# Decode attention on one core: sixteen deferred P V chunks instead of twenty, the next K asked for after piece 9 instead of 13, and wo's last heads ordered by halves

## The chip, the cores and the metric

One core of a Trainium2 chip. The metric is the device time of the whole kernel in microseconds (us), the slowest core's, as a median of several executions. The kernel before takes 1298.5 us; its executions differ by 0.6 us in the first comparison and by up to 2 us in the later ones, so differences of 1 us are read from the traces rather than from the times. Kernels are compared only within the same rounds.

## The reference, cut to what matters

```python
# B, Sq, D = 4, 1, 512;  H, Sk, Dh = 32, 8192, 128;  F = 1792;  all bf16
xn = layernorm(x)
q = (xn @ wq)                                   # [B, H, 1, Dh]
p = softmax(einsum("bhqd,bhkd->bhqk", q, k_cache) * Dh ** -0.5)
o = einsum("bhqk,bhkd->bhqd", p, v_cache)
y = x + o.reshape(B, 1, H * Dh) @ wo + (silu(xn @ w_gate) * (xn @ w_up)) @ w_down
```

K and V are 268 MB each, every byte is used once, and the rest (wq, wo, the three FFN weights) is 14 MB. 551 MB go from HBM to the core whatever the schedule.

## The kernel before

The (b, h) pairs are cut into 32 tiles of four heads. A tile's K is 8.4 MB, its V too, and three slots of that size hold K of the tile at work, V of the one before, and V of the one before that until its last chunk is used; then that slot is free for the next K. All loads go out on SyncE's queue, one DMA for a K or a V.

```python
def t_piece(n, g, jb):      # VectorE: 512 words of K transposed in 32x32 blocks
    kt = kt_pool.tile([P, w // 2], dt.bfloat16, name="kt")         # 3 buffers
    nc.vector.transpose(out=kt[:]..., in_=src[:, :, jb, :])
def s_piece(n, g, jb):      # PE: two matmuls, scores accumulate in PSUM
    for r in range(2):
        mm(s_ps[n][:], zq[:, 2 * jb + r, off:off + P], kt[:, :, r], start=...)
...
for i in range(NT - 1):
    for p in pieces(i, 0, NP):                   # 32 pieces: K of tile i
        if i >= 3 and p in (4, 7, 10, 13):
            pv_to(i - 2, NK - LO + (p - 1) // 3 * (LO // 4))   # LO = 20 chunks left of 64
            if p == 13:
                load_k(i + 1)                    # into V(i-2)'s slot
        if p == 16 and i > 0:
            pt_turn(i - 1)                       # VectorE: 4 transposes of P
    load_v(i)                                    # into K(i)'s slot
    max_1(i); build_q(i + 1)
    pv_to(i - 1, 8); max_2(i)
    ...                                          # each 4th tile: head group closed
    pv_to(i - 1, NK - LO); row_sums(i)
```

A piece is one such transpose with its two matmuls, 32 to a tile; a chunk is one P V matmul, 64 to a tile. `load_k` goes out when the slot is free, that is when PE has done the last P V chunk of two tiles before; where it stands in the program only bounds it.

## Time and profile before

| | before |
|---|---|
| time, median | 1298.5 us (4 runs) |
| DMA busy share, data queue q1 | 99.0% |
| mean rate | 425 GB/s |
| PE / VectorE busy | 85% / 63% |
| data moved | 551 MB |

From the page: the rate in 40 slices, the mean, and the chain of work that ended last; and from the waits, the sum of VectorE's waits for K (total us, times, longest).

```profile
GB/s 420 421 429 445 425 437 431 433 429 435 425 431 423 437 418 427 427 413 443 421 428 427 439 425 419 431 421 437 433 417 429 433 427 431 425 435 429 427 413 309
DMA packets 12612, 551.59 MB, mean 425 GB/s; under 512 B 1276, under 2 KB 1800, under 8 KB 3080
...
DMA 59%; PE 35%; DVE 4%; issue 2%; SPq 0%; ACT 0%; DVEq 0%
```

```profile
DVE kt L278 <- DMA slot<-in_A_k_cache_dram: 55.4, 27, 11.4
```

The rate never leaves 413 to 445 GB/s until the last slice; nothing in it looks like a pause. What 1% can hide is seen only in the records of single DMA packets (start, length, size, queue). Those records do not name the DMA engine.

### The profile page before, as it was taken

The page shows a single profiled execution, that of the slowest core. Times are in us where ns is not written, and L with a number is a line of the kernel's source. Part 1 is how long each engine was busy: PE and PEld are TensorE (multiplying, and loading weights), DVE is VectorE, ACT ScalarE, POOL GpSimd, SP SyncE. Part 2 cuts the span into 40 slices and gives each one's busy share as a digit, 9 for nine tenths or more (in the row PEclk, how much of TensorE's full clock was granted, in tenths as well). Part 3 has the DMA queues.
Part 4 walks back from the last instruction along what each step waited for, and adds up shares of the span by engine and source line. Part 5 has one row for each costly group of instructions (what it writes and reads, how often), then busy time and mean ns, then how long its engine had stood idle before and what let it go on. Part 6 is the DMA issues. An engine that isn't in the chain of part 4 may idle for free.

```text
span 1297.1 us, 12866 instructions
## 1 busy us (share of the span) xinstructions
PE 1099.1 (85%) x5010; PEld 441.8 (34%) x5076; DVE 823.0 (63%) x1509; ACT 34.1 (3%) x79; POOL 3.6 (0%) x11
## 2 busy tenths in 40 slices
PE   1888898988898978888988989878889888889887
PEld 0234333323333323333333333323333233333246
DVE  3956556676557676466776656766566775667753
ACT  1000000000000000000000000000000000000000
POOL 1000000000000000000000000000000000000000
PEclk8897999989989989899989989989999999999887
DMA  9999999999999999999999999999999999999997
GB/s 420 421 429 445 425 437 431 433 429 435 425 431 423 437 418 427 427 413 443 421 428 427 439 425 419 431 421 437 433 417 429 433 427 431 425 435 429 427 413 309
DMA packets 12612, 551.59 MB, mean 425 GB/s; under 512 B 1276, under 2 KB 1800, under 8 KB 3080
## 3 DMA queue, kind: packets, MB, share of 16 engines
q1 hardware_dynamic: 12536, 550.77, 99.0%
q8 instruction: 39, 0.64, 0.2%
q14 instruction: 21, 0.17, 0.0%
q10 hardware_dynamic: 16, 0.01, 0.0%
HBM read 550.77 MB, written 0.00 MB: 425 GB/s over the span
## 4 chain that ended last, share of the span: by engine, by line
DMA 59%; PE 35%; DVE 4%; issue 2%; SPq 0%; ACT 0%; DVEq 0%
DMA slot<-in_A_k_cache_dram 57%; PE sps L75 19%; PE oacc L75 14%; DVE kt L278 4%; DMA slot<-in_A_v_cache_dram 1%; PE mps L75 1%; DVE ptz L315 1%; PE yo_ps L75 1%; PE xps L75 1%; SPq L107 0%; ACT p__385 L306 0%; PE mps L297 0%; DVE rcp L325 0%; DVE mx L291 0%; DVE zq L269 0%
## 5 line engine op out<-in xcount | busy, mean ns | idle before, releaser
L75 PE MATMUL sps<-kt,zq 128*128 128x512 bf16 x1982 | 597.2, 421 | 172.9 <-DVE kt L278 172.3
L278 DVE STREAM_TRANSPOSE kt<-slot 128x512 uint32<-128x512 uint32 x1024 | 639.1, 681 | 152.2 <-PE sps L75 79.7
L75 PE MATMUL oacc<-slot,ptz 128*16 128x512 bf16 x1920 | 457.9, 387 | 0.0
L75 PEld LDWEIGHTS <-zq 128*128 128x128 bf16 x2048 | 202.1, 103 | 542.5 <-issue 397.5
L75 PEld LDWEIGHTS <-ptz 128*16 128x16 bf16 x1920 | 188.9, 107 | 250.1 <-issue 78.0
L325 DVE RECIPROCAL rcp<-mps 128x4 f32<-128x4 f32 x32 | 5.9, 185 | 198.3 <-PE mps L75 198.3
L291 DVE TENSOR_REDUCE mx<-sps 128x1 f32<-128x512 f32 x32 | 22.1, 692 | 23.1 <-PE sps L75 23.1
L75 PEld LDWEIGHTS <-slot 128*128 128x128 bf16 (+1 forms) x658 | 23.3, 110 | 11.6 <-DMA slot<-in_A_v_cache_dram 4.0
L300 DVE TENSOR_REDUCE nm<-mps 128x4 f32<-128x64 f32 x32 | 7.2, 225 | 24.1 <-PE mps L297 24.0
L269 DVE COPY zq<-qt 32x4 bf16<-32x4 bf16 x128 | 21.2, 166 | 1.3
L75 PE MATMUL xps<-ptz,slot 128*128 128x4 bf16 x512 | 15.6, 169 | 3.7 <-DMA slot<-in_A_v_cache_dram 3.7
L371 DVE TENSOR_TENSOR otn<-xps,rcp 32x16 bf16<-32x16 f32 x28 | 4.8, 170 | 21.4 <-PE xps L75 19.3
L75 PEld LDWEIGHTS mps<-rowb,rs 128*128 128x128 f32 x64 | 9.5, 187 | 14.7 <-issue 12.7
L75 PE MATMUL mps<-rowb,rs 128*128 128x4 f32 x64 | 12.3, 263 | 1.7 <-ACT p__385 L306 1.7
L349 DVE TENSOR_TENSOR kt<-kt,rowu 128x512 f32<-128x512 f32 x8 | 5.5, 693 | 10.2 <-ACT kt L348 10.1
L297 PE MATMUL mps<-ident_f,mx 128*128 128x128 f32 x32 | 10.3, 322 | 0.8 <-DVE mx L291 0.8
L75 PEld LDWEIGHTS xps<-rowy,o 128*32 128x32 f32 (+1 forms) x226 | 10.5, 155 | 1.3
L75 PE MATMUL xps<-rowy,o 128*32 128x4 f32 (+1 forms) x226 | 10.3, 203 | 0.0
L297 PEld LDWEIGHTS mps<-ident_f,mx 128*128 128x128 f32 x32 | 4.2, 133 | 13.9 <-DVE zq L269 12.5
L351 DVE TENSOR_REDUCE o<-kt 128x128 f32<-128x512 f32 x8 | 8.3, 1039 | 0.3
L75 PE MATMUL yo_ps<-slot,otn 128*4 128x256 bf16 x64 | 8.1, 290 | 0.3 <-DVE otn L361 0.3
L75 PE MATMUL sps<-slot,xnt_w 128*32 128x512 bf16 x32 | 3.5, 612 | 4.4 <-DMA slot<-in_A_wq_dram 4.4
(148 smaller groups left out, 184.1 us busy)
## 6 DMA issues: line engine op xcount, KB each, us to landing
slot<-in_A_v_cache_dram SPq DMA_DIRECT2D x6, 2048.0 KB, 26.4
slot<-in_A_wq_dram SPq DMA_DIRECT2D x1, 4096.0 KB
slot<-in_A_wo_dram SPq DMA_DIRECT2D x1, 3584.0 KB, 25.8
slot<-in_B_w_gate_dram SPq DMA_DIRECT2D x1, 1792.0 KB, 23.9
slot<-in_B_w_up_dram SPq DMA_DIRECT2D x1, 1792.0 KB, 27.8
slot<-in_B_w_down_dram SPq DMA_DIRECT2D x1, 1792.0 KB, 31.5
slot<-in_A_v_cache_dram SPq DMA_DIRECT2D x1, 1536.0 KB, 14.0
slot<-in_A_v_cache_dram SPq DMA_DIRECT2D x1, 1024.0 KB, 16.1
```

What stands on the lines that cost most here:

```text
L75: nc.tensor.matmul(out_ap, lhsT=lhsT, rhs=rhs, start=start, stop=True, skip_group_check=True, **kw)
L269: nc.vector.tensor_copy(out=zq[a * QB:(a + 1) * QB, :, XO + a * QB].rearrange("p (j r) -> p r j", r=2), in_=qt[a * QB:(a + 1) * QB, half, ...
L278: nc.vector.transpose(out=kt[:].bitcast(dt.uint32).rearrange("p (t r) -> p t r", r=QB), in_=src[:, :, jb, :])
L291: nc.vector.reduce_max(out=mx[:], in_=s_ps[n][:], axis=AX.X)
L297: nc.tensor.matmul(mps[:, 0:P], lhsT=nmx.pop(n)[:, 0:1].to_broadcast([P, P]), rhs=ident_f[:, :], is_transpose=True, start=True, stop=True, ...
L300: nc.vector.tensor_reduce(out=nm[:], in_=by_row(mps[:, 0:P]), axis=AX.X, op=ALU.max, negate=True)
L315: nc.vector.transpose(out=t_[y * QB:(y + 1) * QB, :, y, :, :].rearrange("p s u x -> p s (u x)"), in_=p_[y * QB:(y + 1) * QB, :].rearrange( ...
L325: nc.vector.reciprocal(out=rcp[j][:, :, b], in_=mps[:, P:P + HT])
L349: nc.vector.tensor_tensor(out=o_sb[:], in0=o_sb[:], in1=rowu[:].unsqueeze(2).to_broadcast([P, NV, Dh]), op=ALU.mult)
L351: nc.vector.reduce_sum(out=o1[:], in_=o_sb[:].rearrange("p u d -> p d u"), axis=AX.X)
L371: nc.vector.tensor_tensor(out=otn[q0:q1, j * 4:j * 4 + 4, :], in0=xps[q0:q1], in1=r_[q0:q1, y, :].unsqueeze(1).to_broadcast([QB, 4, B]), o ...
```

## The change

Its intent: the next K is asked for earlier in each tile, so that the DMA queue is never short, and the end is reached sooner because one half of the result is complete earlier.

```diff
-    def wo_mm(i):
-        for half in range(2):
+    def wo_mm(i, halves=(0, 1)):
+        for half in halves:
             mm(yo_ps[half][0:B, :], otn[:, i, :], wo_t[0][...], start=False)
-    LO = 20
+    LO = 16
-            if i >= 3 and p in (4, 7, 10, 13):
-                pv_to(i - 2, NK - LO + (p - 1) // 3 * (LO // 4))
-                if p == 13:
+            if i >= 3 and p in (3, 5, 7, 9):
+                pv_to(i - 2, NK - LO + (p - 1) // 2 * (LO // 4))
+                if p == 9:
                     load_k(i + 1)
-            if p == 16 and i > 0:
+            if p == 12 and i > 0:
                 pt_turn(i - 1)
...
-    wo_ready = H
-    wo_some(H)
-    assert wo_next == H
+    for half in range(2):
+        for h in range(JL * HT, H):
+            wo_mm(h, (half,))
+    assert wo_next == JL * HT
```

## The prediction

> **What bounds the kernel now.** The page's slices come first. DMA is at nine tenths or more in 39 of 40 slices, and PE and DVE are not.
>
> ```profile
> PE   1888898988898978888988989878889888889887
> DVE  3956556676557676466776656766566775667753
> DMA  9999999999999999999999999999999999999997
> ...
> q1 hardware_dynamic: 12536, 550.77, 99.0%
> q8 instruction: 39, 0.64, 0.2%
> q14 instruction: 21, 0.17, 0.0%
> ```
>
> The data queue q1 alone takes 99.0% of 16 engines' span, so all that can be won is in the last per cent: the start, the tail, and places where a DMA engine is slow or has nothing. The chain of waits names K transfers for 57% of the span, but it would do so whether the transfer or its request is late. So I went to the stretch of one tile, first the DMA requests (SyncE's timeline: start, length), then VectorE's wait for K in the same stretch:
>
> ```profile
> 550.24 0.33 SPq L94 DMA_DIRECT2D slot<-in_A_k_cache_dram  x1
> 562.83 0.33 SPq L107 DMA_DIRECT2D slot<-in_A_v_cache_dram  x1
> 588.39 0.33 SPq L94 DMA_DIRECT2D slot<-in_A_k_cache_dram  x1
> 601.71 0.33 SPq L107 DMA_DIRECT2D slot<-in_A_v_cache_dram  x1
> 628.50 0.33 SPq L94 DMA_DIRECT2D slot<-in_A_k_cache_dram  x1
> ...
> 576.05 4.27 DVE L278 STREAM_TRANSPOSE kt<-slot 128x512 uint32<-128x512 uint32 x7 [1.02 <-DMA slot<-in_A_k_cache_dram]
> 614.66 4.31 DVE L278 STREAM_TRANSPOSE kt<-slot 128x512 uint32<-128x512 uint32 x7 [1.78 <-DMA slot<-in_A_k_cache_dram]
> 654.29 4.89 DVE L278 STREAM_TRANSPOSE kt<-slot 128x512 uint32<-128x512 uint32 x7 [2.04 <-DMA slot<-in_A_k_cache_dram]
> ```
>
> The tile period is 38.6 to 39.6 us and VectorE waits 1 to 2 us for K in each, so compute is not the limit. The K landed at 614.66; the V asked for at 601.71 lies behind it and needs some 19.3 us more, until 634. The next K is asked for at 628.50, 5.5 us before that. The V at 601.71 was asked 13 us before its turn. So **only the K requests run near empty**.
>
> The records of single DMA packets say what this costs. A 64 KB packet takes 2.418 us at best, and that is also the median; one engine moves 8 of them per K or V, 19.32 us. Above that minimum, and including gaps, the K windows (from a K request to the next V request) from 157 us on lose 11.9 us per engine on average. It depends on the time from K's arrival to the next K request: 12.3 us loses 0 to 0.14, 13.8 loses 0.5 to 0.8, 14.5 loses 1.3 to 1.7 (the request at 550.24 loses 1.7, that at 588.39 nothing). It looks like a gain of 11 us.
>
> It is not, because **the engines don't run alike**. A transfer's 16 completion records lie 0.8 us apart for the first K, 3 to 4.6 us from 180 us on. I took the third K's 16 completions as zero and subtracted 19.32 us per transfer. After 58 transfers (to K 31) the earliest completion has lost 15.2 us, the last 17.9 us. The earliest loses nearly all of it in K transfers after late requests. The last loses it in 17 steps, most of 0.9 us, one to each of the 8 KB packets of q14 (about one in 66 us): 14.8 us, and q14's packets lie there also where no K is late. Of the other 3.1 us, 1.9 fall in K transfers with a late request (0.5, 0.8, 0.1, 0.2, 0.3) and 1.2 elsewhere. A slot is only ready when the last engine is, so the last engine's 1.9 us are the loss that the time sees; what the others win only puts them further ahead of it.
>
> **What the Trainium skill says.** "DMA: Bandwidth & Descriptors", Specifications, gives a fabric ceiling of 435 GB/s for 16 engines. The trace agrees: 64 KB in 2.418 us on 16 engines are 434 GB/s, and the mean is 425. The same page, "Why a DMA increments its semaphore by 16 and not by 1", says a DMA runs on up to 16 engines "that finish independently", and that only the full count means all data landed; the spread of 0.8 to 4.6 us shows it. Its section "Queues, rings and completion order" says each engine has a ring per queue row, and goes round the rows packet by packet; that fits an instruction packet delaying one engine's data, as the 0.9 us steps suggest. The page "Trainium Kernel Development and Optimization", Key Constraints, says all issuing queues share the same 16 engines, so asking earlier adds no bandwidth; here the busy share of 99% leaves none.
>
> **The change, part by part.** No instruction is added or removed: PE has 9582 rows in both programs, VectorE 336 merged rows in both.
>
> 1. *P V chunks.* Twenty deferred chunks become 16, so four move from a tile's start to the stretch after the previous tile's max. A run of 36 takes 7.96 us, 0.22 each: the stretch grows by 0.9 us. PE's idle before K at 614.66 was 2.77 us, so it is hidden in most tiles; in the one tile in four that closes a head group, whose next tile starts with no wait for K (at 417.83), it delays the start by up to 0.9.
>
> 2. *K's request.* Before, it comes after 13 pieces and 20 chunks: 628.50 - 614.66 = 13.84 us. Now it is after 9 pieces and 16 chunks. The tile's own lines say what a group costs:
>
> ```profile
> 623.09 1.53 PE L75 MATMUL sps<-kt,zq 128*128 128x512 bf16 x6
> 623.75 1.90 DVE L278 STREAM_TRANSPOSE kt<-slot 128x512 uint32<-128x512 uint32 x3 [0.76 <-PE sps L75]
> 624.55 1.26 PE L75 MATMUL oacc<-slot,ptz 128*16 128x512 bf16 x5
> 625.74 1.02 PEld L75 LDWEIGHTS <-zq 128*128 128x128 bf16 x6 [0.42 <-issue]
> ```
>
> Three pieces and five chunks take 625.74 - 623.09 = 2.65 us, about 1.4 + 1.25. Two pieces and four chunks are thus 0.93 + 1.0 = 1.95 us. Three first pieces at 2.8, four chunks at the low clock seen there (2.32 us for five) 1.8, then three groups of 1.95: 10.4 us. So the request comes about 3.4 us earlier after K's arrival. By the table above, 12.3 us was already early enough at a spread of 4 us; at 10.4 us the engines may draw some 7 us apart (4.2 + 13.8 - 10.4 = 7.6) before the fastest waits as at 13.8.
>
> 3. *V's request.* The transpose of P moves from piece 16 to 12 at the same cost (2.85 us on VectorE). Four pieces fewer are slowed by chunks, but the 0.9 us of part 1 is paid elsewhere. V comes perhaps 1 us earlier, where it was 13 us ahead anyway: zero.
>
> 4. *wo by halves.* The last eight matmuls are reordered, so that half 0 is done after four of them. The tail before:
>
> ```profile
> 1292.69 1.86 PE L75 MATMUL yo_ps<-slot,otn 128*4 128x256 bf16 x8 [0.27 <-DVE otn L361]
> 1294.38 0.41 DVE L474 CAST kt<-yo_ps 4x256 bf16<-4x256 f32 x1 [1.74 <-PE yo_ps L75]
> 1294.60 0.36 ACT L476 CAST kt<-yo_ps 4x256 bf16<-4x256 f32 x1 [18.41 <-PE yo_ps L75]
> 1294.82 0.35 SPq L475 DMA_DIRECT2D out_dram<-kt  x1
> 1294.99 0.28 ACTq L477 DMA_DIRECT2D out_dram<-kt  x1
> ```
>
> The VectorE cast and its store start three matmuls earlier, some 3 x 0.2 = 0.6 us. The ScalarE half still waits for the eighth matmul and its store was already the later one, at 1294.99. The end follows that one: 0 to 0.3 us, say 0.1.
>
> The sum: -1.9 (last engine's late-K loss) - 0.1 (tail) = -2.0, so 1298.4 - 2.0 = **1296.4 us**.
>
> **The rivals.** *Request bound:* the K request sets the pace for all engines, and the whole 11.9 us less a remainder of 1 us come back: 1287.5. For it: the 1.7 us at 550.24, the 57% of the chain. Against: the last engine's steps go with q14, not with K's request, and the earliest engine's gain is worth nothing if the last is as late. I give it one chance in ten; half of it, one in seven.
> *Fully hidden:* the slow engine pays q14's packets and nothing else, my 1.9 us are its neighbours' waits: 1298.3. For it: the five steps are small and I can't follow single engines through the records. One in five.
> *Compute takes over:* PE is at 85%, and the tiles that close a head group start without a wait for K (417.83 in VectorE's timeline), so 0.9 us more P V ahead of them, in 7 tiles, could add up to 6 us in all. Against: such a tile is followed by three with 1 to 3 us of wait, V is queued 13 us deep, and the K request in it still comes 2 us earlier than before. It would make 1299 to 1302; one in twenty.
>
> **Range and chances.** The three runs before span 0.6 us. Between hidden (1298.3) and half of the request-bound gain (1293) lies most of the weight: 1292.8 to 1298.7. Faster by over 2% would need 1272.5; 551 MB at 434 GB/s take 1270 us with nothing lost, and some 6 us of tail follow, so that is out of reach. Slower by 2% would need 26 us that nothing here can supply.
>
> **What would show it.** K's request about 10.4 us after K's arrival (13.8 before); V's request within 1 us of before. Slow 64 KB packets after K requests nearly gone; the spread of completions grown from 4 to 6 us or more; VectorE's waits for K (55.4 us before) about the same or longer, since DMA stays the bound; DMA's share no lower than 99%. The last engine's 0.9 us steps stay. In the tail the first cast about 0.6 us before the second. The prediction is wrong if the spread stays at 4 us while the time falls by 5 us or more (the request paced all engines), or if the waits for K vanish (compute took over).

## The result, and the profile after

| | before | after |
|---|---|---|
| first comparison, median | 1298.54 us (4 runs) | 1298.08 us (1297.41 to 1298.92, 4 runs) |
| repeated with five rounds, median | 1299.21 us (9 runs) | 1297.58 us (5 runs) |

Ratios are the mean time of one kernel's runs over that of the other's in the same rounds, so not quite the ratio of the medians: 0.9996 (95% interval 0.9979 to 1.0014) and 0.999 (0.9976 to 1.0003). The kernel is the same within 2%, probably about 1 us faster; no interval excludes zero. The two profiled spans are 1297.1 and 1296.0 us.

The page of the changed kernel, the lines that answer to those before: DMA by slices, queues, chain, and the sum of VectorE's waits for K.

```profile
DMA  9999999999999999999999999999999999999996
GB/s 421 422 429 446 425 440 425 434 435 436 437 427 434 436 429 430 437 422 435 424 421 442 428 419 437 422 437 428 439 426 425 427 423 430 435 425 422 426 411 280
...
q1 hardware_dynamic: 12536, 550.77, 98.9%
q8 instruction: 39, 0.64, 0.2%
q14 instruction: 21, 0.17, 0.0%
...
DMA 65%; PE 29%; DVE 5%; issue 2%; SPq 0%; ACT 0%; DVEq 0%
```

```profile
DVE kt L278 <- DMA slot<-in_A_k_cache_dram: 43.1, 24, 11.4
```

The last slice moves 280 GB/s, 309 before: most engines are done sooner, and one is not, as the packet records will show. First, that the change did what it was to do. The timeline of one tile after, VectorE's start on the new K and SyncE's requests (start, length):

```profile
574.66 3.71 DVE L278 STREAM_TRANSPOSE kt<-slot 128x512 uint32<-128x512 uint32 x6 [1.32 <-DMA slot<-in_A_k_cache_dram]
...
585.65 0.33 SPq L94 DMA_DIRECT2D slot<-in_A_k_cache_dram  x1
601.23 0.33 SPq L107 DMA_DIRECT2D slot<-in_A_v_cache_dram  x1
```

In this tile K is asked for 11.0 us after the last K came (13.8 before), V after 26.6 us (26.4 before). Over 28 tiles, counted from the last completion record of a K, the means are 10.7 us (13.7 before) and 26.3 us (26.8 before).

Now the completions. A K or V transfer writes 16 completion records, one for each DMA engine. As in the prediction, the third K's sorted 16 are zero and 19.32 us are subtracted per transfer; I read the V of tile 29, 57 transfers later (one before the prediction's reading, because the parts of the last V begin to mix after it). These numbers are worked out from the packet records and are no lines of the profile:

| | q14 packets | first engine has lost | last engine has lost | spread of the 16 | K windows lose, mean of engines |
|---|---|---|---|---|---|
| before | 21 | 14.4 us | 17.0 us | 4.5 us | 11.6 us |
| after | 21 | 10.2 us | 16.0 us | 7.4 us | 8.3 us |
| after, repeated | 21 | 9.9 us | 15.0 us | 7.1 us | 7.6 us |

(11.6 us is worked out again, by the way that gives the other two rows; the prediction has 11.9.) The other engines won 4 us, the last one 1 to 2 us, and the time followed the last one. In the changed kernel the last engine stands alone: counted from the earliest of the third K's completions, that is without the zero correction, at that transfer it has lost 17.7 us, the next one 13.1.

That the time follows the last engine can be read directly. From its completion of the V of tile 29 to the landing of the last load it is 69.2 to 69.3 us, and from there to the end of the span 5.4 to 5.5, in the kernel before, in both profiles of the changed one and in runs 1, 2, 6 and 7 below. These spans run from 1295.0 to 1302.9 us, so they differ by what the last engine has lost by then, and by up to 0.4 us in when the third K landed. (In run 5 the first stretch is 69.9 us; with the wide transposes of runs 3, 4 and 8 the two are 69.1 to 70.0 and 6.0 us.)

The tail after, from the last head group to the stores:

```profile
1291.49 1.86 PE L75 MATMUL yo_ps<-slot,otn 128*4 128x256 bf16 x8 [0.27 <-DVE otn L361]
1292.54 0.41 DVE L475 CAST kt<-yo_ps 4x256 bf16<-4x256 f32 x1 [1.10 <-PE yo_ps L75]
1292.98 0.35 SPq L476 DMA_DIRECT2D out_dram<-kt  x1
1293.39 0.36 ACT L477 CAST kt<-yo_ps 4x256 bf16<-4x256 f32 x1 [19.23 <-PE yo_ps L75]
1293.78 0.28 ACTq L478 DMA_DIRECT2D out_dram<-kt  x1
```

The first half is cast 0.85 us before the second, but from the start of these matmuls to the span's end it is 1296.0 - 1291.5 = 4.5 us, and before it was 1297.1 - 1292.7 = 4.4 us. ScalarE's half ends both.

### The profile page after: what moved, and what is told of

Same layout as the page of the kernel before. It is cut to its first block, busy times and chain, and to the rows that moved or that the text cites. A ratio compares the mean times of both kernels' runs of the same rounds, so it can differ in the third digit from the quotient of the medians.

```text
span 1296.0 us, 12866 instructions
## 1 busy us (share of the span) xinstructions
PE 1112.8 (86%) x5010; PEld 441.6 (34%) x5076; DVE 822.0 (63%) x1509; ACT 34.1 (3%) x79; POOL 3.6 (0%) x11
## 3 DMA queue, kind: packets, MB, share of 16 engines
q1 hardware_dynamic: 12536, 550.77, 98.9%
## 4 chain that ended last, share of the span: by engine, by line
DMA 65%; PE 29%; DVE 5%; issue 2%; SPq 0%; ACT 0%; DVEq 0%
DMA slot<-in_A_k_cache_dram 63%; PE sps L75 15%; PE oacc L75 12%; DVE kt L278 4%; DMA slot<-in_A_v_cache_dram 1%; PE mps L75 1%; DVE ptz L315 1%; PE yo_ps L75 1%; PE xps L75 0%; SPq L107 0%; ACT p__385 L306 0%; PE mps L297 0%; DVE rcp L325 0%; DVE mx L291 0%; DVE zq L269 0%
## 5 line engine op out<-in xcount | busy, mean ns | idle before, releaser
L75 PE MATMUL sps<-kt,zq 128*128 128x512 bf16 x1982 | 611.5, 421 | 157.7 <-DVE kt L278 154.1
L349 DVE TENSOR_TENSOR kt<-kt,rowu 128x512 f32<-128x512 f32 x8 | 5.5, 692 | 10.2 <-ACT kt L348 10.1
## 6 DMA issues: line engine op xcount, KB each, us to landing
slot<-in_A_v_cache_dram SPq DMA_DIRECT2D x6, 2048.0 KB, 26.6
```

Source lines behind the costliest of these rows:

```text
L75: nc.tensor.matmul(out_ap, lhsT=lhsT, rhs=rhs, start=start, stop=True, skip_group_check=True, **kw)
L349: nc.vector.tensor_tensor(out=o_sb[:], in0=o_sb[:], in1=rowu[:].unsqueeze(2).to_broadcast([P, NV, Dh]), op=ALU.mult)
```

## The experiments

Ten runs, all correct, numbered as they are told here. The theory to be tested: **one DMA engine, the straggler, sets the time; it loses 0.9 us whenever it also fetches a packet of VectorE's instructions (queue q14), and an earlier K request mainly helps the other 15.** (The expectations give the last engine's loss without the zero correction, 1.4 to 2.7 us more than in my tables and text; what they call "at K 31" was read at the same V of tile 29.) Its rivals: the K request's distance sets the pace (request theory), or compute does (compute theory).

### 1. More VectorE instructions, in its idle time

```diff
+        for c in range(32):
+            nc.vector.memset(dmy[:, c:c + 1], 0.0)      # in each tile, before the long P V
         pv_to(i - 1, NK if i in (1, NT - 2) else NK - LO)
```

> The changed kernel plus 32 one-column memsets per tile on VectorE, put where VectorE waits for P V (7.6 us of idle time), 992 instructions more; nothing else is touched. Straggler theory (one DMA engine alone fetches VectorE's instructions, 128 per 8 KB packet on q14, and loses 0.9 us of its data each time; the other 15 engines don't set the time): q14 grows from 21 packets to about 29, the last engine's loss by 7 us, the time to 1304 to 1306, spread of completions larger. Request theory (the K request's distance sets the pace): VectorE has the idle time, requests unmoved, 1298. Compute theory: 1298 to 1299, with fewer waits for K.

Measured: 1305.42 us against 1298.81 of the kernel before in the same rounds, ratio 1.0055 (1.004 to 1.007). The queue line and the K waits:

```profile
q14 instruction: 29, 0.24, 0.0%
```

```profile
DVE kt L280 <- DMA slot<-in_A_k_cache_dram: 46.8, 24, 11.4
```

Eight packets more for 992 instructions. The last engine lost 22.7 us, 6.7 more than in the changed kernel, and the time is 6.6 us above the kernel before, some 7 to 8 above the changed one, from which it was made. In the profiled spans it is 7.0 (1302.9 against 1296.0). VectorE waits for K no less than in the changed kernel (43.1), and K is asked for 10.9 us after the last K's arrival (10.7), so it wasn't slowed into being the bound. Both rivals expected about 1298.

### 2. The same number of instructions on ScalarE

```diff
-            nc.vector.memset(dmy[:, c:c + 1], 0.0)
+            nc.scalar.copy(out=dmy[:, c:c + 1], in_=rowb[:, 0:1])
```

> Control: the same 992 instructions on ScalarE (tiny copies where it is idle). If any instruction fetch costs the transfers time, 1304 to 1306 as with VectorE. Straggler theory with a fetching engine per compute engine: ScalarE's 8 fetches fall on another DMA engine that has some 5 us of lead, so 1298 to 1299. If ScalarE's fetches fall on the same DMA engine as VectorE's, 1304 to 1306, and the theory narrows to that engine. Request theory: 1298.

Measured: 1298.75 us (before 1298.81), ratio 1.0001 (0.9986 to 1.0015). Its queue line:

```profile
q14 instruction: 29, 0.24, 0.0%
```

The same eight packets on the same queue cost at most 1 us, against 7: the last engine lost 17.0 us, 1.0 more than in the changed kernel's first profile, where the two profiles of that kernel differ by 1.0 themselves. So it isn't fetching as such. The records don't name the engine, but they show whether the last one pays: four of this run's packets (at 529, 684, 806 and 1081 us) have no counterpart in the changed kernel and fall in transfers without another q14 packet, and there the last engine lost 0.00 to 0.09 us. In the transfers with a packet of the other series, which comes about every 66 us as before, it lost 0.84 to 0.99 from 172 us on. ScalarE's fetches thus don't delay the last engine; that another engine with a lead takes them is the reading that fits.

### 3. Half as many transposes, twice as wide

```diff
-    kt_pool = ...(name="ktp", bufs=3)
+    kt_pool = ...(name="ktp", bufs=2)
...
     def t_piece(n, g, jb):
+        if jb == 1:
+            return
-        kt = kt_pool.tile([P, w // 2], dt.bfloat16, name="kt")
+        kt = kt_pool.tile([P, w], dt.bfloat16, name="kt")     # 1024 words
```

(cut: q stays in PSUM in float32, the two halves of the result share a PSUM bank and a few small tiles share buffers, to find the memory)

> The changed kernel with K transposed 1024 words at a time instead of 512: half the transposes and half their extra wait instructions, some 990 VectorE instructions fewer, same bytes, same PE work, same places of the requests (memory found by keeping q in PSUM). Straggler theory: q14 falls from 21 packets to about 13, the last engine loses 7 us less, time 1291 to 1293. Request theory: no change, 1297 to 1299, or slower if the two buffers of twice the size make PE wait. Compute theory: slower, since a first transpose of 1.3 us delays the first scores of each tile by 0.7 us (20 us in all if compute were the bound).

Measured: 1295.00 us, ratio 0.9976 (0.9959 to 0.9993). From the page and the waits:

```profile
q14 instruction: 14, 0.11, 0.0%
...
PE 49%; DMA 24%; DVE 20%; issue 7%; SPq 0%; ACT 0%; DVEq 0%
```

```profile
DVE kt L278 <- DMA slot<-in_A_k_cache_dram: 16.6, 8, 12.1
```

Seven packets fewer, and the last engine lost 10.9 us instead of 16.0. Against the changed kernel the span fell by 3.3 us, less than these 5.1, and by less than expected. The records show where the rest went: the third K lands 0.5 us later (104.5 us against 104.0), from the V of tile 29 to the last load it is 0.7 us more (70.0 against 69.3), and from the last load to the end 0.5 us more (6.0 against 5.5). Of the last, 0.4 us is that the two halves of the result in one bank are cast one after the other (ScalarE's cast starts 2.34 us after the first of the last matmuls, 1.90 in the changed kernel). That compute decides in many tiles is not shown by the chain's 49% for PE: the repeat of the changed kernel has 48% there, its first profile 29%.

### 4. The wide transposes with the instructions given back

```diff
+        for c in range(32):
+            nc.vector.memset((xsum, mean, vsum, rstd)[c % 4][:], 0.0)
```

> Wide transposes (1295.0 us, q14 14 packets) plus 32 four-row memsets per tile on VectorE, again where it waits 8.4 us for P V. Straggler theory: the number of fetches counts and not the size of the transposes, so q14 is back at 21 to 22 packets, the last engine's loss at K 31 goes from 12.3 back to 17.5 to 19 us, and the time to 1299 to 1302, which is the changed kernel's time or a little more. If the wide transposes gained by something else (fewer waits between VectorE and PE), it stays at 1295 to 1296.

Measured: 1301.82 us, ratio 1.0025 (1.0008 to 1.0042); q14 is back at 21 packets and the last engine's loss at 18.1 us. The number of instructions did it, not their width. It ends 4.0 us of span behind the changed kernel with the same number of packets: 2.1 us is the last engine's, 0.7 a later third K, 0.6 lies between the V of tile 29 and the last load, and 0.5 after it. A cause is seen only for the last, the slower tail.

### 5. The K request later

```diff
-            if i >= 3 and p in (3, 5, 7, 9):
-                pv_to(i - 2, NK - LO + (p - 1) // 2 * (LO // 4))
-                if p == 9:
+            if i >= 3 and p in (5, 9, 13, 17):
+                pv_to(i - 2, NK - LO + (p - 1) // 4 * (LO // 4))
+                if p == 17:
-            if p == 12 and i > 0:
+            if p == 20 and i > 0:
```

> The changed kernel with its four groups of four P V chunks beside pieces 5, 9, 13 and 17, so that K is asked for some 17 us after K's arrival (10.4 expected after the change, 13.8 before). Straggler theory: with 19.3 us until V's end the engines can only lie 2 us apart before even the last one is starved; spread of completions shrinks to 1 to 2 us, slow packets after each K request, and the last engine too loses time: 1301 to 1310. Request theory: linear in the request's place, so from the two known kernels (3.4 us earlier brought 0.5 us) about 1299. Compute theory: slower by the same amount in every tile with no K wait at all.

Measured: 1299.96 us (before 1298.81), ratio 1.0012 (0.9997 to 1.0027). A miss in its design: the request came only 1.3 us later than in the kernel before (mean of 28 tiles, from the last completion record), not 3, because four more pieces are partly paid by four chunks fewer. The spread fell to 3.2 us and the first engine lost 16.0 us, as the theory says, but the last one lost 17.2, only 0.2 more than before. The run doesn't reach the region where the last engine starves, and tells the theories apart little.

### 6. The K request earlier still

```diff
-    LO = 16
+    LO = 8
-            if i >= 3 and p in (3, 5, 7, 9):
-                pv_to(i - 2, NK - LO + (p - 1) // 2 * (LO // 4))
-                if p == 9:
+            if i >= 3 and p in (2, 3, 4, 5):
+                pv_to(i - 2, NK - LO + (p - 1) * (LO // 4))
+                if p == 5:
```

> The change pushed further: eight chunks wait instead of 16, two each beside pieces 2, 3, 4 and 5, K asked for after piece 5, some 3 to 4 us earlier again. Straggler theory: the other engines draw further ahead of the last (spread of completions 9 to 11 us instead of 7.5), the last engine's loss at K 31 stays at 17 to 18 us, time 1297.5 to 1298.5, nothing gained. Request theory: another 0.5 us or more, 1297 to 1297.6, and the earliest engine's loss no guide. Compute theory: the eight chunks moved in front of each tile (1.7 us) delay its start, 1299 to 1305.

Measured: 1296.76 us (before 1299.13), ratio 0.9983 (0.9968 to 0.9998). K is asked for 6.9 us after the last K's arrival (10.7 in the changed kernel). It is a little faster than I expected, and the last engine's loss is lower too (16.5 uncorrected, 17 to 18 expected). The first engine has now lost 5.8 us (10.2 in the changed kernel), the spread is 10.7, and the last has lost 15.0, the same as in the changed kernel's repeat. The mean loss in the K windows is 3.9 us, 7.7 us below that of the kernel before; the time fell by 2.4. In this run the last engine's curve is a clean staircase: of its 15.0 us, 14.1 are 16 steps, most of 0.9 us, in transfers with a q14 packet (19 packets in that time; three of them between 702 and 723 us cost it 0.9 us together), while the first engine stays within 0.14 us of zero for 37 of the 57 transfers. What an earlier request can still give the last engine had thus been given in part by the change and is all given here.

### 7. The change without wo's halves

```diff
-    for half in range(2):
-        for h in range(JL * HT, H):
-            wo_mm(h, (half,))
+    wo_ready = H
+    wo_some(H)
```

> The change without its part on wo: the P V chunks and the K request as changed, the last heads of wo head by head as before. The tail of the changed kernel took 4.46 us from the last otn to the end against 4.44 before, so all theories of the loads expect the changed kernel's time, 1297.5 to 1298.5, and a tail of 4.4 to 4.5 us. If the order of wo's halves were worth the 0.6 us by which its first cast came earlier, 1298.6.

Measured: 1297.55 us (before 1299.13), ratio 0.9989 (0.9974 to 1.0004), no slower than the changed kernel. Its tail:

```profile
1291.42 1.87 PE L75 MATMUL yo_ps<-slot,otn 128*4 128x256 bf16 x8 [0.27 <-DVE otn L361]
1293.11 0.41 DVE L474 CAST kt<-yo_ps 4x256 bf16<-4x256 f32 x1 [1.75 <-PE yo_ps L75]
1293.32 0.36 ACT L476 CAST kt<-yo_ps 4x256 bf16<-4x256 f32 x1 [20.95 <-PE yo_ps L75]
```

From 1291.42 to the span's end at 1295.9 it is 4.5 us, as with the halves. ScalarE's cast starts 1.90 us after the first of the eight matmuls in both. The order of the halves is worth nothing.

### 8. A version that beats both, and how far it goes

Wide transposes, with the first and the last of a tile split into two, and the four q copies per tile on ScalarE, whose fetches cost next to nothing in run 2:

```diff
+        if g in (0, NTG - 1):
+            for x in range(2):
+                nc.vector.transpose(out=dj[:, :, x, :], in_=sj[:, :, x, :])
...
-            nc.vector.tensor_copy(out=zq[...], in_=qt[...])
+            nc.scalar.copy(out=zq[...], in_=qt[...])
```

> Wide transposes, with the first and the last one of a tile split into two again (so that PE starts 0.65 us sooner in each tile and ends sooner) and the four q copies per tile moved from VectorE to ScalarE. VectorE's instructions per tile stay about as they were. VectorE's wait for K had fallen to 16.6 us in 8 waits with wide transposes, so compute was close to being the bound. If compute had taken over in part: 1292 to 1294, the K waits back at 20 to 40 us. Straggler alone: q14 stays at 13 to 14, so 1294.5 to 1295.5.

Measured: 1293.04 us (1292.92 to 1293.10, 4 runs; before 1299.13), ratio 0.9954 (0.9939 to 0.9969). q14 stayed at 14 packets and the last engine had lost 10.2 us (10.9 in run 3), and between the third K's landing and the last load both runs have 13 packets: the further 2 us (1.5 in the spans) are not fetches. The latest K request comes 13.7 us after the K's arrival, 14.5 in run 3, so compute may have held the requests back less; that is argued. The K waits are 20.7 us, at the lower edge of what I expected. Then the same with the earlier K request of run 6:

> The wide transposes with split ends and ScalarE's q copies (1293.0 us) together with the earlier K request (1296.8 us against the changed kernel's 1298.1). Straggler theory: the two losses of the last engine are separate (fetches, and neighbours' late K), so about 1 us more: 1291.5 to 1292.5. If compute is the bound by now (8 of 31 tiles wait for K at all), nothing or a loss: 1293 to 1295.

Measured: 1292.98 us (before 1299.21), ratio 0.9953 (0.994 to 0.9965): nothing more. It was run on another chip. The first engine has lost 1.5 us in all and the last one 8.8, 1.4 less than in the run before, and the time doesn't seem to see it. The chain:

```profile
PE 44%; DMA 32%; DVE 15%; issue 8%; ACT 0%; SPq 0%; DVEq 0%; ACTq 0%
```

It belongs to PE and VectorE for more than half, but that doesn't show that compute took over as the bound, since such shares move by some 20 points between two profiles of one kernel (the repeat, below). The packet records say otherwise: in both runs the last load lands at 1285.2 us and the span ends 6.0 us later. Of the 1.4 us, 1.0 is one fetch packet, which falls just before the V of tile 29 is complete in the run before (1213 us) and just after it in this one (1225 us); the rest is taken up by a third K that lands 0.5 us later (105.2 against 104.7). The earlier request won next to nothing for the last engine here. Why, the records don't say, and no run with a faster compute was made.

### The changed kernel repeated

> The changed kernel once more, with more rounds, because its gain (0.5 us in the medians, 1.2 us in the profiles) lies in the noise. Straggler theory, from the last engine's loss at K 31 (18.9 before, 17.7 after): 1.0 to 1.5 us faster than before on the same chip. Fully hidden: within 0.3 us.

Measured: 1297.58 us against 1299.21, the last engine's loss 15.0 us. 1.6 us faster in the medians, but the interval still includes zero. It was run on another chip. The chain of this profile is PE 48% and DMA 45%, where the first profile of the same kernel has 29% and 65%, and the waits for K are 38.7 us. The two spans still differ by what the last engine lost.

## Why the prediction was right or wrong, point by point

- **The number: inside the range, near its upper edge.** 1296.4 us was expected, 1292.8 to 1298.7 the range; measured were 1298.1 and, in the repeat, 1297.6. The first time alone lies nearer to the "fully hidden" rival (1298.3), so the times don't show the mechanism; the traces do.
- **What bounds the kernel: right.** The data queue stayed at 98.9% and the time at 1298. Of 11.6 us lost after K requests, 3.3 were won back (4.0 in the repeat) and the time gave about 1; in run 6 it was 7.7 and 2.4. That is what the prediction meant by an apparent gain that is none.
- **The straggler: right, and shown.** More VectorE instructions lengthened the span by 7.0 us for 8 packets, 0.9 us each; fewer shortened it; the same number on ScalarE did next to nothing. The steps of 0.9 us stayed, and the spread grew to 7.4 us, as forecast. One step for every q14 packet is not quite right: ScalarE's packets make none in the last engine (run 2).
- **The term "-1.9, last engine's late-K loss": the right term, a little too large for this change.** The last engine won 1.0 us in one profile and 2.0 in the other; the times say 0.5 and 1.6. I had assumed that the change takes away all late-K loss. It doesn't, for the next reason; in run 6, which takes away most of it, the last engine won 2.0.
- **"Slow 64 KB packets after K requests nearly gone": wrong.** They are nearly gone until 480 us (0.4 us of loss, 3.2 before). By 515 us the completions lie 7.3 us apart, the first engine finds the queue short again, and the loss returns: 8.3 us of the 11.6 remain. The prediction names this limit (7.6 us apart) in its second part and forgets it in its list of signs. The request moved the point at which the leaders are held back from 4.5 to 7.4 us.
- **K's request at 10.4 us: 11.0 measured in the tile shown, 10.7 as the mean of 28.** The sum of pieces and chunks was 0.3 to 0.6 us short.
- **V's request up to 1 us earlier: about half of it.** It came at 26.3 us instead of 26.8 in the mean (26.5 in the repeat; in the tile shown 0.2 later). No run tests alone what it was worth.
- **VectorE's waits for K "about the same or longer": wrong.** They fell from 55.4 to 43.1 us. Four more chunks of P V, 0.9 us, now stand between a tile's scores and the next tile, so VectorE probably comes to its wait later, while K itself comes at nearly the same time.
- **The tail, 0.1 us: it was zero.** The first cast came 0.85 us before the second (0.6 expected), but the second one ends the kernel, and run 7 shows no loss without the reordering.
- **The rivals.** The request-bound one (1287.5) fell with run 6: an even earlier request gave 2.4 us in all. "Fully hidden" (1298.3) is what the first times look like, and the repeat speaks against it. Compute did not take over in this kernel, although VectorE waits for K only 24 times (19 in the repeat, 27 before): the span still follows the last engine's completions. With fewer fetches no run shows that it did.

What stays open: why a fetch packet whose own record is 0.31 us long costs the data of its engine 0.9 us, which engine it is, and why the earlier request won nothing more with wide transposes.

## What to carry to other kernels

With DMA at 99%, as here, the mean over 16 engines no longer tells what an earlier request is worth. Look at the completion records of single transfers: if they lie several us apart, the time may follow the last engine, as it did here, and what the others win only makes them idle at the end. Then ask what that engine does besides the data; here it fetched one compute engine's instructions, and fewer, wider instructions brought the kernel 6 us below the one before (with what the change itself and the split ends gave), where the best place tried for the request alone brought 2.4.

## What the Trainium skill lacked or had wrong

- "Runtime: NRT & Kernel Launch", Instruction fetch mechanics: it says that instructions are refilled in 16 KiB blocks of 256 and that crossing a boundary is "mostly hidden". PE's fetches, on q8, agree (39 packets of 16 KB for some 10,100 instructions); VectorE's and ScalarE's are 8 KB, and 992 instructions more made 8 packets more. In this kernel, bound by DMA, VectorE's are not hidden: 0.9 us of time for each.
- None of the pages read says which DMA engine fetches for which compute engine. The runs show that it matters for whom a packet is fetched: the same 8 packets cost 7 us from VectorE and at most 1 from ScalarE.
- "DMA: Bandwidth & Descriptors", Latency and other measured facts, gives slow engines in traces as a matter of two fixed engines, with a best guess about rings that GpSimd's DMAs use. This kernel issues no DMA from GpSimd, and one engine (which one, the records don't say) still fell 16 us behind, 14 of them by instruction fetches.
- None of the pages read gives the cost of a request that comes just before the queue runs dry. Here, after the K request at 550.24 us, a third of the 64 KB packets took 2.6 to 3.9 us instead of 2.418, and with the gaps it was 1.7 us per engine.
